# Denser filler matmuls on TensorE in a linear-attention, Fourier-mixing and feed-forward kernel

## The chip, the cores and the metric

The kernel runs on one core of one Trainium2 chip. The metric is the device time of one execution in microseconds (us); lower is better. Everything is float32, apart from the weights, which arrive as float64 and are split into two float32 parts on the core.

## The reference

Three steps follow one another. For 4 batches of 8 heads, a gated recurrence over 768 tokens with a 48 x 48 state; then for each batch the real part of a two-dimensional Fourier transform (768 tokens by 384 channels), added to its input; then a normalization and a feed-forward network of width 1536 with a residual.

```python
for t in range(S):
    state = alpha[:, :, t, :, None] * state + np.einsum('bhd,bhe->bhde', k[:, :, t], v[:, :, t])
    y[:, :, t] = np.einsum('bhd,bhde->bhe', q[:, :, t], state)
...
X = np.fft.fft(x, axis=1)
X = np.fft.fft(X, axis=2)
u = x + np.real(X).astype(np.float32)
un = (u - mu) / np.sqrt(var + 1e-06)
ch = np.maximum(un @ w_ch1, 0.0) @ w_ch2
return (u + ch).astype(np.float32)
```

## The kernel before

The work goes batch by batch. Attention runs over pairs of heads, four pairs to a batch: VectorE (DVE) makes running products of alpha by scans and multiplies them into k and q (tiles `al` and `w`), TensorE (PE) transposes one of them (`a<-cst,al`, evacuated into `kt`), forms the scores of 128 tokens by 128 (`w,al`: one matmul with 64 rows for one head and one with 48 for the other), ScalarE (ACT) evacuates them, GpSimd (POOL) masks them, and PE multiplies them with v (`vn`, or `wt` where a weight buffer is lent to v) and adds the state that came from earlier tokens (`tt`). The Fourier step folds the outputs on DVE (`z<-f`), does one transform by matmuls with constants (`cst,z`) and the second by matmuls with more constants (`cst,x`), and DVE adds the result to `y`, normalizes it (`st`, `mv`, `r`) and writes `f`, which PE transposes (`cst,f`). The feed-forward network has matmuls `x,wt` into the hidden layer `h` and `wt,h` out of it; both operands are split into two parts, and three products are kept. The first batch has no feed-forward work to lie beside its attention; from the second batch on, the attention of a batch is woven into the feed-forward matmuls of the batch before.

The order on each engine is written ahead of time. Every operation is recorded as an `Op` with its dependences, and `Plan.emit` places the operations one by one on planned clocks of the engines, from a table of estimated durations (`duration`), latencies between engines (`LAT`) and sort keys. An operand that comes to PE from another engine is planned `MARGIN` (1.0 us) later than its estimate, for all but the feed-forward matmuls (`u.fill`). The planned times serve for the order alone: on the chip an engine takes its next instruction as soon as the semaphores that it waits for allow it. Nearly all instructions therefore have one source line, L465, the line of the recorded call; L210 is the ReLU.

One kind of instruction is not an operation of the plan. Where PE's planned clock stands still until time `t`, the emitter writes filler matmuls into PE's instruction stream ahead of the operation, as many as the planned idle time holds steps of `DUMMY`, as long as `t` is under `WARM`. They multiply a tile of zeros (`zero`, 128 x 32, with itself) into 32 unused columns of a PSUM buffer, `f2` number 2, and nobody reads the result. They stand in the profile as line L1111, `f<-zero`. They take no planned time, so that the plan does not depend on how many there are. As a filler is an ordinary instruction of PE's queue, the operation behind it starts after it, whether its own operands have come or not.

```python
if op.engine == "PE" and self.idle and t < self.idle[2] and not self.open:
    for _ in range(int((t - max(clock["PE"], self.idle[1])) / DUMMY)):
        order.append(self.idle[0])
...
plan.idle = (lambda: nc.tensor.matmul(warm[2][0:32, 480:512], zero.real(), zero.real(), start=True, stop=True), 1.0, WARM, ("f2", 2))
```

Loads of alpha (`al`) go through SyncE's queue into four buffers; the load for a later pair waits until PE has read the buffer for the last time. `c` is a check of the loaded alphas on ACT (`ACT c<-al`), which DVE waits for before it uses the tile.

Of the kernel before, what the change touches and what calls it, by code (L numbers as in the profile page):

```python
# [51 lines left out]
SPLIT = 388  # L52
KCK = -700.0
KF0 = -505.0
WARM = 120.0
MARGIN = 1.0
DUMMY = 0.11
KTINY = 0.5 * 2.0**15 / (1.0 + 15.5 / 128.0)


# [113 lines left out]
class Plan:  # L174
# [177 lines left out]
    def emit(self):  # L352
# [35 lines left out]
        while placed < len(ops):  # L388
# [35 lines left out]
# [3 lines that stand above are left out]
# [56 lines left out]
def gla_mix_ffn(ctx: ExitStack, tc: tile.TileContext, alpha, kq, v, w1, w2, consts, rowtab, out):  # L483
# [625 lines left out]
    warm = plan.tags["f2"]["reals"]  # L1109
    if WARM:  # L1110
        plan.idle = (lambda: nc.tensor.matmul(warm[2][0:32, 480:512], zero.real(), zero.real(), start=True, stop=True), 1.0, WARM, ("f2", 2))  # L1111
    with tc.manual_schedule():
# [147 lines left out]
```

## Time and profile before

| | |
|---|---|
| median of 3 runs | 569.54 us (565.82 to 577.62) |
| the profiled execution | 569.96 us, span 568.2 us from the first to the last instruction |
| PE busy | 541.2 us, 95% of the span |
| DVE busy | 370.1 us, 65% |
| ACT busy | 170.6 us, 30% |
| POOL busy | 63.6 us, 11% |
| mean granted TensorE clock | 0.944 |
| DMA | 42.23 MB, mean 74 GB/s |
| fillers (L1111) | 946 matmul records from 1.0 to 117.0 us |

The profile is of one execution. It gives for each engine its busy time, for PE the share of the full clock that was granted (PEclk), for each idle stretch what ended it, and a chain of work followed back from the last instruction. PE stands for matmuls and PEld for the weight loads that go with them. The ends of matmuls are modelled, so where matmuls follow closely, the distance from one group's start to the next group's start is the better measure of what a group costs. A PE that is busy with fillers is busy in these tables too.

### The profile page before, as it was taken

Reading aid. Unit: us, or ns where it says so; the run is one execution under the profiler, and the core shown is the slowest. Engines: PE = TensorE matmul, PEld = TensorE weight load, DVE = VectorE, ACT = ScalarE, POOL = GpSimd, SP = SyncE. Lnnn points to the kernel's source line nnn. Section 1 sums busy time; section 2 is a strip of 40 time slices with the busy share of each in tenths; the row PEclk is TensorE's granted clock in tenths of the full one; section 3 lists DMA queues with packets and bytes.
Section 4 is the critical chain, followed back from the end, with each engine's and each line's share of the span. In section 5 each row is a group of like instructions: output and inputs, shape, how many; then the busy total and the mean of one; then the engine's idle time right before and its main releaser. Section 6 shows DMA issues by size and latency. Waiting matters only on the chain.

```text
span 568.2 us, 10337 instructions
## 1 busy us (share of the span) xinstructions
PE 541.2 (95%) x4220; PEld 519.8 (91%) x4220; DVE 370.1 (65%) x952; ACT 170.6 (30%) x373; POOL 63.6 (11%) x81
## 2 busy tenths in 40 slices
PE   6999979869999999989999999999999999999995
PEld 6899979758999999979999999999999999999995
DVE  6548799977699789996757995467564922312111
ACT  2354513342555413144233221233312211211110
POOL 0111251010102310003122000021220000000000
PEclk9558988787999999999999999999999999999999
DMA  8995371020320151113244200102010100100001
GB/s 221 283 367 133 155 270 31 1 74 3 91 73 0 31 162 35 43 42 80 90 133 146 77 31 1 42 1 71 23 58 28 42 1 2 42 1 15 28 1 46
DMA packets 16549, 42.23 MB, mean 74 GB/s; under 512 B 1904, under 2 KB 7088, under 8 KB 16496
## 3 DMA queue, kind: packets, MB, share of 16 engines
q1 hardware_dynamic: 15440, 39.08, 21.9%
q0 software_dynamic: 768, 2.36, 1.4%
q8 instruction: 35, 0.57, 0.4%
q14 instruction: 18, 0.15, 0.1%
q10 hardware_dynamic: 288, 0.07, 0.1%
HBM read 34.42 MB, written 7.08 MB: 73 GB/s over the span
## 4 chain that ended last, share of the span: by engine, by line
PE 86%; DVE 7%; DMA 3%; ACT 2%; issue 1%; SPq 1%; ACTq 0%
PE f L465 58%; PE a L465 25%; DMA al<-in_alpha_dram 3%; PE f L1111 3%; DVE y L465 2%; DVE x L465 1%; DVE wt L465 1%; SPq L465 1%; DVE st L465 1%; ACT c L465 1%; DVE z L465 0%; DVE tt L465 0%; DVE h L465 0%; DVE w L465 0%; DVE al L465 0%
## 5 line engine op out<-in xcount | busy, mean ns | idle before, releaser
L465 PE MATMUL f<-x,wt 128*128 128x384 f32 x864 | 180.8, 347 | 2.1 <-DVE x L465 1.8
L465 PE MATMUL f<-wt,h 128*128 128x384 f32 x864 | 177.3, 344 | 0.3 <-ACT h L210 0.3
L465 PEld LDWEIGHTS f<-x,wt 128*128 128x128 f32 x864 | 153.1, 191 | 4.6 <-DVE x L465 2.1
L465 PEld LDWEIGHTS f<-wt,h 128*128 128x128 f32 x864 | 151.7, 189 | 1.7 <-ACT h L210 0.6
L465 DVE SCALAR_TENSOR_TENSOR h<-f,h 128x384 fp32r<-128x384 f32 x96 | 53.1, 554 | 106.0 <-ACT h L210 105.0
L210 ACT ACTIVATE h<-f 128x384 fp32r<-128x384 f32 x96 | 47.2, 492 | 197.5 <-PE f L465 194.7
L465 POOL TENSOR_SCALAR_AFFINE_SELECT w<-w 128x384 f32<-128x384 f32 x64 | 42.4, 682 | 290.9 <-ACT w L465 290.8
L465 PE MATMUL a<-vn,w 128*128 128x64 f32 x312 | 49.3, 287 | 0.3 <-ACT kt L465 0.3
L465 PEld LDWEIGHTS a<-vn,w 128*128 128x128 f32 x312 | 46.2, 209 | 0.9 <-issue 0.4
L1111 PEld LDWEIGHTS f<-zero 128*32 128x32 f32 x946 | 37.3, 124 | 4.9 <-issue 2.0
L1111 PE MATMUL f<-zero 128*32 128x32 f32 x946 | 40.4, 209 | 1.2 <-DVE zero L465 1.0
L465 ACT COPY w<-a 128x384 f32<-128x384 f32 (+4 forms) x58 | 26.2, 481 | 35.2 <-PE a L465 33.9
L465 DVE TENSOR_TENSOR_SCAN w<-al,d 112x768 f32<-112x768 f32 (+1 forms) x17 | 28.6, 1680 | 12.4 <-PE a L465 8.1
L465 DVE TENSOR_TENSOR y<-y,a 128x191 f32<-128x191 f32 (+2 forms) x96 | 28.5, 345 | 8.3 <-PE a L465 8.1
L465 PE MATMUL a<-w,al 48*128 48x128 f32 (+1 forms) x276 | 33.7, 296 | 0.0
L465 PEld LDWEIGHTS a<-w,al 48*128 48x128 f32 (+1 forms) x276 | 27.5, 193 | 4.1 <-issue 1.6
L465 DVE TENSOR_TENSOR sd<-y,y 128x288 f32<-128x288 f32 x32 | 13.2, 453 | 25.0 <-ACT y L465 25.0
L465 DVE TENSOR_TENSOR_SCAN al<-al,d 112x768 f32<-112x768 f32 (+1 forms) x17 | 28.2, 1656 | 0.0
L465 PE MATMUL a<-tt,w 112*128 112x96 f32 x134 | 27.8, 295 | 0.0
L465 DVE TENSOR_TENSOR y<-y,f 128x384 f32<-128x384 f32 (+2 forms) x44 | 21.2, 515 | 6.9 <-PE f L465 6.7
L465 PEld LDWEIGHTS a<-tt,w 112*128 112x128 f32 x134 | 22.6, 203 | 0.9 <-issue 0.2
L465 POOL DMA_INDIRECT y<-scr,rows x12 | 18.1, 1510 | 46.1 <-DMA scr<-y 33.5
(121 smaller groups left out, 576.7 us busy)
## 6 DMA issues: line engine op xcount, KB each, us to landing
kq<-in_kq_dram SPq DMA_DIRECT2D x13, 672.0 KB, 5.2
wt<-in_w_dram SPq DMA_DIRECT2D x8, 768.0 KB, 10.6
al<-in_alpha_dram SPq DMA_DIRECT2D x15, 336.0 KB, 5.3
out_dram<-y SPq DMA_DIRECT2D x24, 192.0 KB, 1.9
vn<-in_v_dram SPq DMA_DIRECT2D x14, 296.0 KB, 3.1
wt<-in_w_dram SPq DMA_DIRECT2D x8, 384.0 KB, 9.2
scr<-y SPq DMA_DIRECT2D x4, 576.0 KB, 3.7
wt<-in_kq_dram SPq DMA_DIRECT2D x2, 672.0 KB, 14.8
```

The source lines that it names most:

```text
L210: return lambda out, x: e.activation(out, x, AF.Relu)
L465: op.ins = op.fns[op.engine](*[real(a) for a in op.args], **{k: real(x) for k, x in op.kwargs.items()})
L1111: plan.idle = (lambda: nc.tensor.matmul(warm[2][0:32, 480:512], zero.real(), zero.real(), start=True, stop=True), 1.0, WARM, ("f2", 2))
```

## The change

Two constants of the plan change. `DUMMY`, the step by which planned idle time of PE is divided into fillers, goes from 0.11 to 0.04 us, and `WARM`, the planned time up to which fillers are written at all, goes from 120 to 150 us.

```diff
-WARM = 120.0
+WARM = 150.0
 MARGIN = 1.0
-DUMMY = 0.11
+DUMMY = 0.04
```

All other instructions stand in the same order on all engines as before. PE's queue alone differs, in the number of fillers at each place. Ahead of its first work PE had, and has (`a_44` is the first transpose of alpha, `f_0_49` the first product of v with `kt`, and `f_0_47` and `f_1_48` the first scores):

```order
L1111 MATMUL f_2_51_116<-zero 32x32 x61
L465 MATMUL a_44_109<-cst,al_36_101 128x112 x3
L1111 MATMUL f_2_51_116<-zero 32x32 x20
L465 MATMUL f_0_49_114<-vn_42_107,kt_6_71 112x96 x3
L465 MATMUL f_0_47_112<-w_1_2_67,al_36_101 128x128
L465 MATMUL f_1_48_113<-w_1_2_67,al_36_101 128x128
```

```order
L1111 MATMUL f_2_51_116<-zero 32x32 x170
L465 MATMUL a_44_109<-cst,al_36_101 128x112 x3
L1111 MATMUL f_2_51_116<-zero 32x32 x55
L465 MATMUL f_0_49_114<-vn_42_107,kt_6_71 112x96 x3
L1111 MATMUL f_2_51_116<-zero 32x32
L465 MATMUL f_0_47_112<-w_1_2_67,al_36_101 128x128
```

The 61 and 20 fillers became 170 and 55, and one stands behind the product with v.

In the first batch's second transform (`a_139`, `f_1_140` and `a_141` are the three row blocks of the result, and `f_0_143` is the first transpose of the normalized rows) PE's queue before had:

```order
L465 MATMUL f_1_140_1067<-cst,x_17_82 128x97
L1111 MATMUL f_2_137_1026<-zero 32x32 x45
L465 MATMUL a_141_1134<-cst,x_18_83 128x96
L465 MATMUL a_141_1134<-cst,x_18_83 128x95
L465 MATMUL a_141_1134<-cst,x_17_82 128x96
L465 MATMUL a_141_1134<-cst,x_17_82 128x97
L1111 MATMUL f_2_137_1026<-zero 32x32 x70
L465 MATMUL f_0_143_1248<-cst,f_142_1169 128x128
```

and has with the change:

```order
L465 MATMUL f_1_140_1693<-cst,x_17_82 128x97
L1111 MATMUL f_2_137_1627<-zero 32x32 x125
L465 MATMUL a_141_1840<-cst,x_18_83 128x96
L465 MATMUL a_141_1840<-cst,x_18_83 128x95
L465 MATMUL a_141_1840<-cst,x_17_82 128x96
L465 MATMUL a_141_1840<-cst,x_17_82 128x97
L1111 MATMUL f_2_137_1627<-zero 32x32 x194
L465 MATMUL f_0_143_2078<-cst,f_142_1875 128x128
```

Here 45 and 70 became 125 and 194. The other large place is ahead of the first transform (`cst,z`), where 98 became 271. Summed up over PE's queue, with the time at which each stretch lay in the profile before:

| stretch of PE's queue (us before) | fillers before | fillers now |
|---|---|---|
| up to the first product with v (12.96) | 81 | 225 |
| 12.96 to 45.65 | 48 | 144 |
| 45.65 to 72.42 | 103 | 291 |
| 72.42 to the first transform (82.02) | 98 | 271 |
| 82.02 to the first transpose of `f` (104.43) | 129 | 358 |
| after 104.43 | 14 | 46 |
| all | 473 | 1335 |

Of the last row, one before and six now stand behind the matmuls that free an alpha buffer at 116.3 us; there is none further on.

## The prediction

> **What bounds the kernel now.** I read the page first: its slices in time, and under them the shares of the chain that ended last.
>
> ```profile
> PE   6999979869999999989999999999999999999995
> DVE  6548799977699789996757995467564922312111
> PEclk9558988787999999999999999999999999999999
> ...
> PE 86%; DVE 7%; DMA 3%; ACT 2%; issue 1%; SPq 1%; ACTq 0%
> ```
>
> A slice is 14.2 us. PE is busy from end to end and carries 86% of the chain. Its clock is full but in the first ten slices, and there the fillers lie too. So I cut the span where the clock changes. The columns are PE, PEld, DVE, ACT and POOL busy with counts, then the granted clock, DMA share and GB/s.
>
> ```profile
> 1.04:13.30 12.26, 8.40 (x168) 8.10 (x169) 8.81 (x40) 3.02 (x6) 0.00 (x0) 1.00 0.90 238
> 13.30:47.40 34.10, 34.10 (x261) 30.54 (x260) 19.60 (x52) 14.89 (x34) 3.98 (x8) 0.50 1.03 312
> 47.40:81.60 34.20, 31.41 (x531) 29.15 (x528) 28.27 (x68) 13.74 (x27) 9.14 (x9) 1.00 0.47 166
> 81.60:88.40 6.80, 6.38 (x33) 6.41 (x34) 5.50 (x12) 2.23 (x4) 4.46 (x3) 0.50 0.68 218
> ...
> 105.50:115.70 10.20, 10.14 (x62) 8.58 (x62) 8.03 (x17) 5.83 (x11) 1.30 (x1) 0.50 0.01 2
> ...
> 125.90:136.20 10.30, 7.25 (x27) 7.25 (x27) 9.41 (x22) 2.43 (x7) 0.00 (x0) 0.50 0.00 0
> 136.20:568.20 432.00, 422.09 (x2793) 410.13 (x2791) 265.71 (x672) 120.19 (x267) 41.68 (x54) 1.00 0.15 47
> ```
>
> Four stretches have half the clock. The long last one, with 2793 matmuls, has the full clock and no filler. What PE waited for in it, and then in the part ahead of it:
>
> ```profile
> PE f L465 <- DVE x L465: 1.8, 1, 1.8
> PE a L465 <- DVE x L465: 1.1, 2, 0.9
> ...
> PE f L465 <- DVE tt L465: 6.7, 1, 6.7
> PE f L465 <- ACT kt L465: 3.9, 1, 3.9
> PE f L465 <- issue: 3.2, 1, 3.2
> PE f L465 <- DVE f L465: 2.1, 1, 2.1
> ```
>
> After 136 us PE waits some 4 us in all, so whatever moves the start of that stretch moves the end by nearly as much. The whole question is when PE gets there. Before it, PE has 15.9 us of waits, four cold stretches, and its fillers. The same windows for line L1111 alone (PE and PEld):
>
> ```profile
> 13.30:47.40 34.10, 8.55 (x129) 7.48 (x130) 0.50 1.03 312
> ...
> 81.60:88.40 6.80, 0.00 (x0) 0.00 (x0) 0.50 0.68 218
> ...
> 105.50:115.70 10.20, 1.91 (x24) 1.51 (x24) 0.50 0.01 2
> ...
> sum 568.20, PE 40.37 PEld 37.34; mean PE 4.04 PEld 3.73
> ```
>
> The fillers take 40.4 us of PE, and all of it lies ahead of the bound stretch.
>
> **The change part by part.** It adds 862 fillers (473 to 1335) and moves nothing else. Each is queued ahead of real work on the engine that sets the end, so a filler is free only as far as the instruction behind it would have waited anyway. Three terms follow: what the fillers cost, what the warmer clock gives back, and what of the fillers lies in waits that PE has already.
>
> First their price, from PE's instructions in order of time (start, length, group). One filler in the queue is two matmul records here: 61 stand first in the queue, and 122 in the trace.
>
> ```profile
> 1.04 6.25 PE L1111 MATMUL f<-zero 128*32 128x32 f32 x122 [1.04 <-DVE zero L465]
> ...
> 23.51 1.60 PE L1111 MATMUL f<-zero 128*32 128x32 f32 x26
> 25.04 0.69 PE L465 MATMUL a<-vn,w 128*128 128x64 f32 x2
> ...
> 72.42 6.39 PE L1111 MATMUL f<-zero 128*32 128x32 f32 x196
> ...
> 97.72 4.62 PE L1111 MATMUL f<-zero 128*32 128x32 f32 x140
> ```
>
> At full clock 98 fillers took 6.39 us and 70 took 4.62: 65 ns each. At half clock 13 took 25.04 - 23.51 = 1.53 us, 118 ns each. The first 61 took 6.25 us, 102 ns each: PE starts cold. I take 65 ns for all, and 37 ns more for the first 61, as they were: 1335 x 0.065 + 61 x 0.037 = 86.8 + 2.3 = 89.1 us. That is **48.7 us more** than 40.4. The step of 0.04 us by which they are counted is thus not what one costs: a planned microsecond of idle time gets 25 fillers, which run 1.63 us. At the old step it got 9, which run 0.59.
>
> Second, the clock. The same kind of matmul, ten of them, in a cold and in a full-clock stretch, each with the group behind it:
>
> ```profile
> 35.79 2.18 PE L465 MATMUL a<-vn,kt 128*112 128x96 f32 x10
> 37.90 1.33 PE L1111 MATMUL f<-zero 128*32 128x32 f32 x21
> ...
> 64.25 1.15 PE L465 MATMUL a<-wt,kt 128*112 128x96 f32 x10
> 65.23 0.39 PE L465 MATMUL f<-tt,w 112*128 112x96 f32 x2
> ```
>
> From start to start it is 2.11 us against 0.98, so full clock saves 54% of the cold real work. That work is 34.10 - 8.55 = 25.6 us in the first cold stretch, 6.4 in the second and 10.14 - 1.91 = 8.2 in the third: 40.2 us, of which full clock saves **21.5**. I take the whole of it. The cold stretches begin at 13.3, 81.6 and 105.5, behind PE's idle times of 3.9, 3.2 and 2.1 us, and these are just where the fillers become most numerous. Between 47.4 and 81.6 the same mix of attention and fillers kept the full clock.
>
> [...]
>
> Third, the waits. The 3.9, 3.2 and 2.1 us (**9.2 us**) each lie right behind a group of fillers, and fillers take their place. Does anything wait behind them for PE? At 82.02 PE waits for the folded `z`, at 104.43 for the normalized `f`:
>
> ```profile
> 81.08 2.91 DVE L465 TENSOR_TENSOR z<-f 128x576 f32<-128x576 f32 x6
> ...
> 103.90 0.47 DVE L465 TENSOR_SCALAR f<-y,mv,r 128x384 f32<-128x384 f32 x1
> ```
>
> DVE delivers the first `z` near 82 us, so 3.2 us after the fillers ran out. But 98 became 271, that is 173 x 0.065 = 11.2 us against a gap of 3.2. Ahead of `f`, 45 and 70 became 125 and 194: 13.3 us against 2.1. At the start 81 became 225, 144 x 0.065 = 9.4 us against 3.9 (the cold first ones are in both). So each gap is overfilled, and PE, not DVE, is late behind it.
>
> The sum: 48.7 - 21.5 - 9.2 = **18.0 us later** when PE comes to the next point, 116.3 us. Step by step, with real cold work divided by 2.15: the first `vn,kt` comes at about 18.2 (12.96 before), the point 45.65 at 40 (PE is ahead there, the clock pays), 72.42 at 78, the first transform at 95 (82.02), the first transpose of `f` at 127 (104.43), and 116.3 at 134 to 135. What is late from there is a chain that the fillers don't touch:
>
> ```profile
> 116.03 0.28 PE a L465 x3
> ...
> 116.32 3.49 DMA al<-in_alpha_dram
> 119.81 0.02 issue
> 119.83 1.03 ACT c L465 x2
> 120.86 0.73 ACT wt L465
> ...
> 121.62 0.96 DVE wt L465
> ...
> 128.33 0.57 DVE tt L465
> ...
> 128.95 10.85 PE f L465 x48
> ```
>
> PE's last read of an alpha buffer at 116.31 lets the load go, 3.5 us; ACT checks it, DVE has 7.3 us of work in line, and only then has PE its `tt`. All of it starts from PE and takes 12.6 us wherever it lies, with 6 fillers in it where 1 was. So I leave PE's wait of 6.7 us and the cold stretch behind it as they are. Span 568.2 + 18.0 = 586.2; the profiled execution had 569.96 - 568.2 = 1.8 us around its span, which gives **588**. The profiled execution is 0.4 us over the median of the runs, which changes nothing.
>
> **The rivals.**
>
> *The chain at 116 closes up.* If DVE, idle while PE runs fillers, has the work ahead of `tt` done sooner, the wait of 6.7 us goes, and with it the cold stretch that follows (7.25 x 0.54 = 3.9): 588 - 10.6 = 577. For it: the 194 fillers ahead of `f` take 12.6 us, and DVE's work beside them took 6.7 (97.72 to 104.43), so DVE runs ahead there. Against it: DVE's order is fixed and the load waits for PE. 0.11.
>
> *The fillers are cheap, and the kernel gets faster.* One mechanism, the price of a filler in long groups. The gain from clock and gaps is 30.7 us, so the sum is even at (86.8 - 18.0) / 1335 = 52 ns. At the planned 40 ns it is 1335 x 0.025 = 33.4 us less: 554, or 564 if the gaps then stay open. Against it: the two longest groups, 98 and 70 in a row, ran at 65 and 66 ns, no less than short ones. 0.05, with the next case in it.
>
> [...]
>
> *The clock does not hold.* If PE falls back to half clock after the first fillers and stays there until 45.65, as before, the 13.7 us are not saved, and the 144 fillers there cost 0.053 more each, 7.6: 588 + 21 = 609. For it: attention alone did not lift the clock for 34 us. Against it: 47.4 to 81.6 held it. 0.06.
>
> *Nothing happens*, since the fillers lie in idle time only: this needs PE to wait behind them, and the four waits ahead of 136 us sum to 15.9 us, less than 48.7. I give it nothing of its own.
>
> **How the numbers follow.** The forecast has 0.78. Its own spread: filler prices from 64 to 67 ns are -1.3 to +2.7 us, the phase of the first clock change +-2, and up to 9.2 us if new waits open where I fill all: 581 to 598. The range reaches down to the first rival, 577 to 598. A kernel of this spread (565.82 to 577.62) can tell about 2% from no change: 2% over 569.54 is 580.9. The forecast and the clock rival are beyond it (0.84), the first rival and the 568 of the floor within (0.13), cheaper fillers faster (0.03).
>
> **What would show it.** L1111 with 2670 records and 85 to 92 us of PE; a clock of 1.00 from about 7 to 140 us; PE's waits of 3.9, 3.2 and 2.1 gone, the one for `tt` of some 6.5 us still there; the first transform at 95 and the transposes of `f` at 127 us, with DVE idle ahead of its `y` additions. A stretch at half clock between 15 and 45 us, or a filler under 60 ns in the long groups, would prove the sum wrong, and a span under 577 the whole of it.

## The result, and the profile after

| | before | with the change |
|---|---|---|
| median | 570.08 us | 604.96 us (603.75 to 605.36) |
| ratio, with 95% interval | | 1.0635 [1.0574, 1.0696] |
| span of the profiled execution | 568.2 us | 603.6 us |
| mean granted clock | 0.944 | 0.987 |

The change made the kernel 6.4% slower. The forecast was 588 us, within 577 to 598: the right sign, and half the size. Executions of one kernel fall into a faster and a slower group, so every ratio in this document compares the faster groups alone, while the medians are over all executions (one of 2,686 us without fillers among them).

The page of the kernel after, in 40 slices as before, then its chain and its line for the fillers:

```profile
PE   7799998999699999998999999999999999999995
PEclk9899999999899999998999999999999999999999
DMA  8993408000204003411234430012002100100101
...
PE f L465 54%; PE a L465 23%; PE f L1111 15%; DMA al<-in_alpha_dram 2%; DVE y L465 1%; DVE x L465 1%; DVE wt L465 0%; DVE w L465 0%; DVE h L465 0%; DVE al L465 0%; ACT c L465 0%; ACT kt L465 0%; ACT h L210 0%; SPq L465 0%; DVE f L465 0%
...
L1111 PE MATMUL f<-zero 128*32 128x32 f32 x2670 | 93.6, 198 | 9.9 <-issue 8.7
```

The clock did what it was to do: from 4.5 us on it is full up to 161 us, but for one window (21.6 to 25.0). The price is in the chain: fillers carry 15% of it (2.7% before). And the last line has something that the kernel before did not have: fillers themselves wait, 8.7 us, for "issue", that is for nothing that the profile shows. PE's waits by the one waited for:

```profile
PE f L1111 <- issue: 8.7, 4, 3.5
PE f L465 <- DVE tt L465: 5.9, 1, 5.9
```

The waits of 3.9, 3.2 and 2.1 us for `kt`, `z` and `f` are gone, and that for `tt` is still there. In their place stand four stops inside filler groups. PE in order of time shows them:

```profile
1.04 8.65 PE L1111 MATMUL f<-zero 128*32 128x32 f32 x223 [1.04 <-DVE zero L465]
13.07 3.86 PE L1111 MATMUL f<-zero 128*32 128x32 f32 x117 [3.38 <-issue]
16.86 0.51 PE L465 MATMUL a<-cst,al 112*128 112x112 f32 x3
17.30 0.44 PE L1111 MATMUL f<-zero 128*32 128x32 f32 x8
21.21 4.80 PE L1111 MATMUL f<-zero 128*32 128x32 f32 x102 [3.47 <-issue]
25.95 0.83 PE L465 MATMUL f<-vn,kt 128*112 128x96 f32 x6
...
90.14 8.67 PE L1111 MATMUL f<-zero 128*32 128x32 f32 x268
100.08 4.21 PE L1111 MATMUL f<-zero 128*32 128x32 f32 x128 [1.26 <-issue]
104.91 4.78 PE L1111 MATMUL f<-zero 128*32 128x32 f32 x146 [0.61 <-issue]
...
128.93 12.47 PE L1111 MATMUL f<-zero 128*32 128x32 f32 x388
141.33 0.55 PE L465 MATMUL f<-cst,f 128*128 128x128 f32 x3
```

The stops come in the middle of one group of like instructions, and what ended them is no semaphore that the profile shows: after 111 fillers at the start, after four in the second group. The group of 194 at 128.93 runs through. What is different is seen in the windows (PE, PEld, DVE, ACT, POOL; then clock, DMA share, GB/s):

```profile
9.70:13.07 3.37, 0.00 (x1) 0.00 (x0) 1.44 (x5) 2.06 (x2) 0.00 (x0) 1.00 1.00 240
13.07:17.70 4.63, 4.63 (x128) 4.38 (x127) 4.18 (x9) 0.55 (x3) 0.00 (x0) 1.00 1.03 248
17.70:21.20 3.50, 0.04 (x2) 0.00 (x0) 0.18 (x1) 1.45 (x5) 0.00 (x0) 1.00 1.06 255
...
98.80:100.10 1.30, 0.04 (x2) 0.02 (x1) 1.30 (x4) 0.00 (x0) 1.30 (x1) 1.00 1.03 409
...
128.00:141.30 13.30, 13.30 (x396) 13.19 (x396) 9.60 (x38) 0.59 (x2) 0.00 (x0) 1.00 0.01 4
```

Three of the four stops, 8.1 of the 8.7 us, lie where the 16 DMA engines are full (share 1.00 to 1.06); the share over the fourth is 0.57, but it was 1.00 from 98.78 to 102.39 us, just ahead of it. The group at 128.93 runs through where they are idle (0.01). Full DMA engines alone do not stop PE: from 5.0 to 9.7 us fillers ran on beside a share of 1.04. That the missing thing is PE's instructions themselves follows from the queue that brings them. The page before has, as packets, MB and share,

```profile
q8 instruction: 35, 0.57, 0.4%
```

against

```profile
q8 instruction: 49, 0.80, 0.6%
```

on the page after: 14 packets more of 16 KB, 229 KB for 862 fillers of two weight loads and two matmuls: some 67 bytes per instruction (all 49 packets are of 16 KB), so a packet holds 61 fillers or a few more, 4 us of work for PE. By the packets' times in the trace, those of this queue landed at 11.65, 19.91, 98.78 and 103.50 us, and PE went on at 13.07, 21.21, 100.08 and 104.91: 1.3 to 1.4 us behind each.

How far PE gets between two stops says the same. Counted in the trace, matmuls, weight loads and the few semaphore instructions of its queue together, PE ran exactly 256 instructions from 13.07 to its next stop at 17.74 us, 256 from 21.21 to 28.68, and 256 from 100.08 to 104.29. A packet of 16 KB divided by 256 is 64 bytes, or 64 fillers to a packet: PE used up one packet and stood until the next was there. The stop at 28.68 is not among fillers at all. It is 0.42 us in the midst of scores, and PE went on 1.3 us behind the packet that landed at 27.82:

```profile
27.86 0.82 PE L465 MATMUL f<-w,al 48*128 48x128 f32 x9
29.10 0.82 PE L465 MATMUL f<-w,al 48*128 48x128 f32 x9 [0.42 <-issue]
```

Where the 35.4 us of span came from, up to the last read of the alpha buffer (116.3 before, 150.6 after, 34.3 later), in the terms of the prediction:

| term | forecast | measured |
|---|---|---|
| busy time of fillers | +48.7 | +53.2 (93.6 - 40.4) |
| stops inside filler groups | 0 | +8.7 |
| cold real work at full clock | -21.5 | -17.9 |
| waits of 3.9, 3.2 and 2.1 | -9.2 | -9.2 |
| sum | 18.0 | 34.8 |

The measured saving of 17.9 is the sum, over the stretches between filler groups, of the time that the same real matmuls took in both traces (68.1 and 50.2 us).

### The profile page after: what moved, and what is told of

It is laid out like the page before. It is cut to its first block, busy times and chain, and to the rows that moved or that the text cites. A ratio compares the mean times of both kernels' runs of the same rounds, so it can differ in the third digit from the quotient of the medians.

```text
span 603.6 us, 13785 instructions
## 1 busy us (share of the span) xinstructions
PE 576.7 (96%) x5944; PEld 556.5 (92%) x5944; DVE 372.1 (62%) x952; ACT 170.6 (28%) x373; POOL 63.0 (10%) x81
## 4 chain that ended last, share of the span: by engine, by line
PE 92%; DVE 3%; issue 2%; DMA 2%; ACT 1%; SPq 0%; ACTq 0%
PE f L465 54%; PE a L465 23%; PE f L1111 15%; DMA al<-in_alpha_dram 2%; DVE y L465 1%; DVE x L465 1%; DVE wt L465 0%; DVE w L465 0%; DVE h L465 0%; DVE al L465 0%; ACT c L465 0%; ACT kt L465 0%; ACT h L210 0%; SPq L465 0%; DVE f L465 0%
## 5 line engine op out<-in xcount | busy, mean ns | idle before, releaser
L465 DVE SCALAR_TENSOR_TENSOR h<-f,h 128x384 fp32r<-128x384 f32 x96 | 53.2, 555 | 106.1 <-ACT h L210 105.2
L1111 PE MATMUL f<-zero 128*32 128x32 f32 x2670 | 93.6, 198 | 9.9 <-issue 8.7
L1111 PEld LDWEIGHTS f<-zero 128*32 128x32 f32 x2670 | 89.9, 115 | 13.6 <-issue 9.8
L465 PE MATMUL a<-vn,w 128*128 128x64 f32 x312 | 45.0, 268 | 0.3 <-ACT kt L465 0.3
L465 PEld LDWEIGHTS a<-vn,w 128*128 128x128 f32 x312 | 42.0, 191 | 0.7 <-issue 0.4
L465 PEld LDWEIGHTS a<-w,al 48*128 48x128 f32 (+1 forms) x276 | 26.4, 187 | 4.1 <-issue 1.6
L465 PE MATMUL a<-tt,w 112*128 112x96 f32 x134 | 26.2, 282 | 0.0
L465 POOL DMA_INDIRECT y<-scr,rows x12 | 18.2, 1518 | 50.7 <-DMA scr<-y 38.1
L465 ACT COPY y<-a 128x288 f32<-128x288 f32 x27 | 10.8, 399 | 40.5 <-PE a L465 40.3
```

Source lines behind the costliest of these rows:

```text
L465: op.ins = op.fns[op.engine](*[real(a) for a in op.args], **{k: real(x) for k, x in op.kwargs.items()})
```

## The experiments

Theory A, formed on this trace: a filler beyond a wait costs its own time, and a dense group of them also uses up PE's instructions faster than the instruction queue brings new ones while the loads fill the DMA engines. All ratios are to the kernel before, which ran beside them on the same chip.

| run | fillers | median, us | ratio [95% interval] |
|---|---|---|---|
| none | 0 | 570.4 | 0.9907 [0.9848, 0.9965] |
| price065 | 815 | 573.18 | 1.0037 [0.9983, 1.0092] |
| start_only | 617 | 581.65 | 1.0248 [1.0159, 1.0337] |
| late_old | 849 | 584.78 | 1.0284 [1.0210, 1.0357] |
| no_start | 1191 | 599.99 | 1.0575 [1.0480, 1.0669] |
| wide | 401, other kind | 701.71 | 1.2237 [1.2162, 1.2312] |
| sized | 190, other kind | 609.23 | 1.0652 [1.0600, 1.0705] |
| traffic | 1335 | 613.34 (one run) | |
| sized_narrow | 541 | 567.83 | 0.9906 [0.9838, 0.9975] |
| sized_attn | 593 | 566.53 | 0.9912 [0.9863, 0.9962] |

`WARM` got no run: the last planned wait that gets fillers ends at 98 planned us, under both bounds, so by the listing of the emitter it changes nothing.

### Is it the instruction queue?

`traffic` adds load where there was none. One copy from memory to memory is issued when the first transform has been evacuated; nobody waits for it.

```diff
+    nc.sync.dma_start(extra_small[0 : x.shape[0], :], x)
+    nc.sync.dma_start(extra_big[:, :], w1.bitcast(I32))
```

> The changed kernel with one more copy of 4.7 MB from memory to memory, which starts when ScalarE has evacuated the last block of the first transform (near 115 us) and nobody waits for, so that the load queues are full beside the groups of 125 and 194 fillers, which ran without a stop (120 to 141 us). Theory A: idle times of 0.5 to 3.5 us inside these groups, about one for every 64 fillers, and the transposes of f come 5 to 12 us later. Rival C (the stops belong to the program's start and to instructions that run for the first time, not to the loads): both groups run through as before.

PE beside the copy in order of time (the fillers have line L1115 here), and then two windows of it:

```profile
121.13 7.12 PE L1115 MATMUL f<-zero 128*32 128x32 f32 x219
132.98 1.81 PE L1115 MATMUL f<-zero 128*32 128x32 f32 x31 [4.72 <-issue]
134.72 2.02 PE L465 MATMUL a<-cst,x 96*128 96x96 f32 x8
136.68 14.21 PE L1115 MATMUL f<-zero 128*32 128x32 f32 x388
```

```profile
120.00:128.20 8.20, 8.20 (x230) 8.08 (x230) 6.15 (x22) 0.00 (x0) 0.00 (x0) 1.00 1.06 356
128.20:133.00 4.80, 0.08 (x3) 0.02 (x1) 0.00 (x0) 0.00 (x0) 0.00 (x0) 0.77 0.63 218
```

The group of 125 ran in 8.0 us without a stop in the kernel after; beside the copy it stops for 4.7. It stops once, behind 110 fillers, not once per 64: one packet had landed at 121.83, early in the group. The next took until 131.70 to land, and PE went on 1.3 us later. (The share of 0.63 is a mean over the stop; up to 130.54, when that packet started, it was 1.01.) Before the next group the copy was over, and that group ran through. Rival C is out: the same fillers at the same place, and only the load is new. Stops and work also alternate here as before: 256 instructions each from 13.62 to 19.68, from 21.88 to 29.19 and from 101.66 to 105.87 us. The transposes of `f` came at 150.8 in place of 141.3, 9.5 us later, 1.3 of it already there at the first transform; besides the stop, the clock fell to half behind it (0.50 from 133.0 to 136.6).

`wide` takes instructions away: the fillers load 128 columns of zeros in place of 32, with fewer instructions per us.

```diff
-    zero = fixed([P, 32], "zero")
+    zero = fixed([P, P], "zero")
-nc.tensor.matmul(warm[2][0:32, 480:512], zero.real(), zero.real(), ...)
+nc.tensor.matmul(warm[2][:, 480:512], zero.real(), zero.real()[:, 0:32], ...)
-DUMMY = 0.04
+DUMMY = 0.13
```

> The fillers load 128 columns of zeros as weights in place of 32, so that one filler should take about 0.2 us with the same four instructions, and the step is 0.13 (some 400 fillers) so that their time on PE is about that of the change. Theory A (a dense group runs PE out of instructions while the load queues are full): a third of the instructions per us, so no idle time inside a filler group at 10, 18 and 99 to 105 us, the first product with v at about 19, and 594 to 598 us in all. Rival B (what stops the groups there is not the number of instructions but PE's access to memory beside the loads): idle times of the same 3.4, 3.5 and 1.3 us in the same places, 605 us.

No group stops, though those at the start run beside full loads; that half is as theory A has it. It does not rule out rival B by itself, since these fillers, at half clock, also read memory more slowly (2 x 160 columns in 426 ns, against 2 x 64 in 65); the 256 instructions between stops do. The 594 to 598 us were far off, for a reason that neither theory had. PE in order of time, and a window:

```profile
143.66 35.52 PE L1111 MATMUL f<-zero 128*128 128x32 f32 x166
178.99 3.24 PE L465 MATMUL f<-cst,z 128*97 128x65 f32 x16
...
186.66 2.87 PE L1111 MATMUL f<-zero 128*128 128x32 f32 x24
189.36 1.41 PE L465 MATMUL a<-cst,x 96*128 96x96 f32 x8
```

```profile
143.66:178.00 34.34, 34.34 (x163) 34.34 (x162) 12.46 (x25) 2.26 (x4) 8.30 (x3) 1.00 0.36 124
```

83 fillers (166 records) took 178.99 - 143.66 = 35.3 us, 426 ns each; 12 of them at 186.66 took 2.70, 225 ns each. The first are at half clock. (The window says 1.00, but the trace has its first clock record at 183.2 us, and the profile takes what lies ahead of the first record as full. The distance of like matmuls is the surer sign.) So PE was busy without a gap for 34 us, matmul and weight load both 34.34 of 34.34, and half clock stayed. The fillers of the change, in dense groups at the start, do lift it (full from 4.5 us): they move as many columns as they load, these a quarter. That wide fillers do not lift the clock is shown, here and by `sized` below. That it is the share of moved columns that counts is not shown: attention matmuls that move 64 to 128 columns for 112 or 128 loaded, with small groups of the change's own fillers among them, also left PE busy without a gap at half clock, for 27 us in `start_only` (58.6 to 85.9).

### Which fillers cost, and what they are worth

`no_start` gives the first two places their old number, `start_only` gives only them the new one, `late_old` gives the old number to everything behind the first batch's attention. Each replaces the divisor in the emitter's loop:

```diff
-int((t - max(clock["PE"], self.idle[1])) / DUMMY)
+int((t - max(clock["PE"], self.idle[1])) / (0.11 if t < 10.5 else DUMMY))   # no_start
+int((t - max(clock["PE"], self.idle[1])) / (DUMMY if t < 10.5 else 0.11))   # start_only
+int((t - max(clock["PE"], self.idle[1])) / (DUMMY if t < 50 else 0.11))     # late_old
```

> Step 0.11 for the fillers ahead of the first product with v (81 of them, as before the change), step 0.04 behind it: 1191 fillers in all. Theory A (a dense filler group starves PE of instructions while the load queues are full): the stalls of 3.4 and 3.5 us at 9.7 and 17.7 us go, the first product with v is back near 13 us, and the two small stalls near 100 us stay. Whether the 144 fillers from 13 to 45 us then hold the clock is open: if they lift it, about 592 us; if half clock stays until the 157-filler group, about 605 to 610. Rival B (a filler's own time is all, the idle times in the groups are something that any filler meets): the time falls by the 144 x 0.065 = 9.4 us alone, and an idle time of some us is still seen inside a filler group ahead of 26 us.

It measured 600, 8 above the 592 for a lifted clock, though the clock was lifted, at 21.7 us. The first product with v came at 14.0 us and the two stops at the start went, which rival B does not allow; one of 0.9 us came at 27.2, and of the two near 100 us one stayed, 1.3 us. But theory A's own effect came up at a new place: with PE earlier, the group of 157 now lies beside loads. PE in order of time, and a window:

```profile
43.83 4.38 PE L1111 MATMUL f<-zero 128*32 128x32 f32 x133
51.34 6.90 PE L1111 MATMUL f<-zero 128*32 128x32 f32 x169 [3.13 <-issue]
```

```profile
45.00:48.20 3.20, 3.20 (x102) 3.13 (x99) 3.20 (x7) 1.05 (x3) 0.00 (x0) 1.00 1.04 230
```

The same 157 fillers had no stop in the kernel after, at 52 us, when the loads were over (share 0.04 from 50 to 62). It is a second place where the same fillers stop beside loads and run through without them, though here they also come at another time.

> Step 0.04 ahead of the first product with v (225 fillers), 0.11 behind it: 617 in all. Theory A: the two stalls at 9.7 and 17.7 us are there with some 7 us, the first product with v comes at 26 us, and the clock is full from there; real work to 50 us then takes 15 us and fillers 7, so the point that lay at 50.1 us comes at 48 to 50, and the time is that of the kernel before, 565 to 572. Rival B (the loss sits in the groups behind 50 us alone, and the start costs nothing because its work waits for loads anyway): below 560.

The point that lay at 50.1 us came at 50.11: 13.0 us lost at the start, all won back at full clock by then, as theory A had it. The rest missed: 581.65 against 565 to 572, and rival B's time below 560 is further off still. Behind it lie only the old 392 fillers, and the clock fell, as its windows show.

```profile
50.00:58.60 8.60, 6.74 (x63) 5.73 (x64) 8.60 (x24) 4.10 (x8) 4.91 (x2) 1.00 0.59 185
58.60:85.90 27.30, 27.30 (x184) 25.28 (x184) 11.47 (x29) 7.64 (x15) 5.28 (x7) 0.50 0.14 55
```

In 50 to 58.6 us PE was idle for 1.9 us, and half clock followed for 27 us in which it was busy all the time. The kernel before ran the same matmuls at full clock (47.4 to 81.6). Whether the clock holds there is thus not settled by the number of fillers.

> Step 0.04 up to a planned time of 50 us (through the group of 157 and the attention behind it), 0.11 from there: the groups of 64, 271, 39, 125 and 194 go back to 23, 98, 14, 45 and 70, about 475 fillers fewer. Theory A (each filler beyond a wait puts PE, and so the end, back by its own 65 ns, and the stalls come from full load queues): 31 us of fillers and the stalls of 1.9 us near 100 us go, the waits of 3.2 and 2.1 us ahead of the two Fourier steps come back: 577 to 581 us. Rival D (once the first groups have put PE 13 us back, DVE is ahead, and the later groups lie in time that PE would lose anyway): over 590.

584.78 lies between the two, 4 us above theory A's range and 5 below rival D's 590. The groups of 98, 45 and 70 were back, 486 fillers fewer than in the change, and with them came the waits of 3.2 and 2.5 us and the two cold windows behind them, which the forecast had left out (real work 5 us longer from 82 to 116).

> Step 0.065 everywhere, the measured price of a filler at full clock: some 815 fillers, so that a planned idle microsecond holds one microsecond of fillers. If overfilling (fillers that run longer than the planned gap) is the larger part of the loss: 520 fillers fewer are 34 us less, about 571 to 576, and one stall of 3 to 4 us at 9.7 us is left. If stalls and the planned gaps themselves are the larger part: over 585.

573.18 and no difference from before. With a step of the fillers' real price the loss is gone, so overfilling is its larger part. Not one stop is left but three, of 2.0, 2.1 and 1.5 us, in the profiled execution (586.14 us).

> No fillers at all. If the clock depends on them: half clock in nearly all of the first 136 us, real work there some 90 us in place of 68, waits for DVE in between, 575 to 590 us. If the 473 fillers of the kernel before buy nothing: 560 to 570.

Without any filler the kernel is no slower: its ratio is 0.9907. The interval ends under 1, but the difference is less than the 2% that this spread can tell. PE's waits in it:

```profile
PE f L465 <- DVE f L465: 11.3, 1, 11.3
PE f L465 <- issue: 9.1, 1, 9.1
PE f L465 <- DVE tt L465: 7.1, 1, 7.1
PE a L465 <- DVE al L465: 7.1, 1, 7.1
PE f L465 <- ACT kt L465: 5.6, 1, 5.6
PE a L465 <- DVE tt L465: 3.4, 1, 3.4
```

This is the room that fillers have: 7.1, 5.6, 3.4, 9.1 and 11.3, 36.5 us at the five large places (7.1 us for `tt` get no fillers). At these places the change put 972 fillers, which with their stops took 74 us, and 363 more elsewhere. And the 473 fillers of the kernel before buy nothing either: real work is cold to 88 us without them, but PE comes to the transposes of `f` at 107 us against 104, and to 136 us 0.7 us later, inside the spread.

### A version by the waits

The room was first filled with the wide fillers of `wide`. `sized` has 190 of them, 28 and 24 ahead of the first product with v and 41 ahead of the first transform, counted at what they cost at full clock. The forecast was 553 to 562 us if they held the clock, 562 to 570 if not. It measured 609.23, far outside both. The clock has its first record at 128.55 us, and the first 28 fillers took 12.0 us, 427 ns each as at half clock in `wide`: each took twice what it was counted for. PE came to the first transform at 124.4 us, against 85.3 without any filler. So wide fillers kept PE busy for 126.9 of the first 128 us and did not lift the clock.

With the change's own fillers, and the room again taken at its word, `sized_narrow` has 58, 75, 46, 120, 14, 0 and 120 fillers at the large places and step 0.11 in attention.

```diff
-int((t - max(clock["PE"], self.idle[1])) / DUMMY)
+int((t - max(clock["PE"], self.idle[1])) / STEP.get(round(max(clock["PE"], self.idle[1]), 1), 0.11))
+STEP = {1.0: 0.116, 8.1: 0.030, 29.4: 0.136, 56.9: 0.090, 76.2: 99.0, 82.1: 0.065}
```

(The steps stand rounded here.)

> The change's own fillers (32 columns), in number by the waits that PE has in the kernel without fillers: 58 and 75 ahead of the first product with v (waits of 7.1 and 5.6 us), 46 where PE waits 3.4 us, 120 ahead of the first transform (9.1 us), 14, none and 120 in the second (11.3 us), step 0.11 in attention: some 525 in all. Theory A: no group runs past its wait by more than 1 us, one stall of 0 to 2 us at 10 us. If these fillers hold the clock from 13 us on, cold real work of 26 us there takes 15 and the time is 552 to 562 us. If the clock is lost in attention all the same, or DVE sets the pace once PE is quicker: 562 to 570, no better than without fillers.

0.9906. No group overran by much, and the first product with v came at 13.4 us at full clock. Then, by the windows, the clock was lost in attention:

```profile
13.40:19.50 6.10, 4.92 (x60) 4.12 (x60) 5.66 (x14) 3.54 (x11) 1.86 (x4) 1.00 1.04 257
19.50:46.80 27.30, 27.30 (x222) 24.95 (x222) 15.88 (x40) 11.49 (x25) 2.15 (x5) 0.50 1.03 319
```

`sized_attn` has step 0.065 there and 60 in place of 46.

```diff
-/ STEP.get(...)
+/ (0.065 if 10.5 < t < 27 else STEP.get(...))
```

> The fillers of sized_narrow, whose clock fell to half at 19.5 us, in attention: step 0.065 there in place of 0.11 (some 84 fillers where it had 48, about 2.5 us more) and 60 in place of 46 ahead of the first long wait. If the clock then holds from 13 us to the first transform: 26 us of cold work in 15, less 3 us of fillers, 555 to 562 us, and faster than the kernel without fillers. If it falls to half all the same (too little streaming between the groups, or a wait in between), or DVE sets the pace at 80 us: 563 to 570, no better.

0.9912, no better. Its profiled execution (568.88 us, above the median) held the clock from 4.8 to 52.6 us and was 7.7 us ahead at the point of 50.1; then half clock came, to 76.5, and at the first transform it was 4.4 us behind. Without fillers and with the narrow fillers by the waits, the ratio is 0.99 all three times, the intervals lie on one another, and none differs from the kernel before by the 2% that can be told here. The plainest of them, `WARM = 0`, is no worse and is the version to keep.

## Why the prediction was right or wrong

**Right.** What bounds the kernel: the end moved with the start of the long stretch, 33.3 us later at 136 us before, 35.4 at the end. The price of a filler: the group of 271 took 19.5 us with 1.9 of stops in it, 65 ns each, as used. The three waits vanished, the one for `tt` stayed (5.9 for 6.5 forecast), and the chain behind the alpha buffer took 12.6 us again, from 150.60 to 163.19. The rival of that chain closing up did not come about, nor did a clock that does not hold up to 45.65 (its 13.7 us are 25.6 x 0.54), nor fillers cheap enough to gain: no long group behind the start has them under 63 ns. The 568 us in the sum of the chances is for a filler of 50 ns (588 - 1335 x 0.015), a price that no run shows: in the kernel after the long groups behind the start took 64 to 66 ns a filler.

**Wrong: "a filler is free only as far as the instruction behind it would have waited", with the price as its only cost.** The sum had no term for the instructions themselves. The text ahead of the prediction has an engine take its next instruction as soon as its semaphores allow; the stops, each of which ended 1.3 to 1.4 us behind a packet of the instruction queue, show that the instruction must have been fetched as well. Four stops, 8.7 us, are the largest part of the miss of 16.8. The first product with v was forecast for 18.2 us and came at 26.0: 6.9 of the 7.8 us are the first two stops. The rows that could have warned were in the profile before: DMA share 0.90 up to 13.3 us, where 144 fillers were added, and 1.03 behind it, where 96 were, and the instruction packets as a DMA queue of their own.

**Wrong in size: "full clock saves 54%" of all cold work.** One pair of groups, `vn,kt` against `wt,kt`, gave the ratio. Over all real work from the first product with v to the point of 50.1 us it was 26.4 us against 15.1, 43%. The forecast for the point 45.65, 40 us, missed by 11.8 (51.8): 7.8 from the start, the rest from here and from the price. The prediction also set its cold stretches behind PE's idle times of 3.9, 3.2 and 2.1 us. As a cause those are loose at best: with the change the clock stayed full through the stop of 3.38 us at 9.7, and it fell behind idle times of 2.1 us in the kernel before (102.34 to 104.43) and of 1.75 in `start_only` (56.7 to 58.5). That idle time alone sets it is not shown here.

**Wrong in size: 48.7 us more of fillers.** It was 53.2, because not every filler runs at the price of a long group. Of the 4.5 us, 3.2 come from 169 fillers in groups of under 20, which kept PE busy for 84 ns each. Most of the rest is second-hand: behind the stop at 17.7 us the clock was at half from 21.6 to 25.0, and the 51 fillers there took 93 ns each.

The range ended at 598 because the largest loss allowed for was 9 us of new waits. The stops alone would have used that up.

## What to carry to other kernels

A filler is an instruction of the queue: size it by the wait that the profile shows without it, at its measured price (65 ns here), because what stands behind it pays for those too many: with 520 fewer (`price065`) the ratio was 1.0037 in place of 1.0635. Before keeping an engine busy for the sake of its clock, run the kernel without the fillers; here 473 of them bought nothing, and 1335 cost 6%. A long run of short instructions also has to be fetched: 8.1 of the 8.7 us for which the fillers stood still lay beside full DMA engines, so look at their share beside it.

## What the runs showed of the hardware

Two things were not expected. PE's instructions come through a DMA queue in packets of 16 KB, and a dense run of short matmuls (64 fillers to a packet, 4 us) outruns it when the DMA engines are full (share 1.00 to 1.06 over three of the four stops of the kernel after): 19 stops of over 0.3 us inside filler groups in six kernels, 0.3 to 4.7 us long, each ending 1.3 to 1.7 us after such a packet landed, and where one stop follows soon on another, 256 instructions after it. And PE's busy time in the records does not by itself free the clock: 34 us of back-to-back fillers with 128 columns of weights and 32 moved columns, both PE rows at 100%, left it at half (426 ns a filler, 225 at full clock), while the dense groups of fillers with 32 and 32 brought it to full 4.5 us after the program's start, and 6.5 in the kernel before; without fillers it was at half up to 88.9 us (ten `wt,kt` took 1.97 us at 50.9 us, against 0.98 at full clock).
